# Pooling the first batch's keys with a 0/1 matrix of 32 columns in place of the identity

## The chip, the cores and the metric

The kernel runs on one core of a Trainium2 chip. A core has a matrix engine, TensorE (PE in the profile, with its loads of the stationary operand shown apart as PEld), three engines for elementwise work and reductions (VectorE or DVE, ScalarE or ACT, GpSimd or POOL) and sixteen DMA engines, whose transfers this kernel issues from SyncE's queue (SP). The engines run side by side, each in the order in which its instructions were written, and wait for each other through semaphores.

The metric is the device time of one execution. The kernel before takes 1979.55 us, the median of three runs from 1979.36 to 1980.42 us.

## The reference

```python
kv_pool = kv.reshape(B, H // r, r, W // r, r, C).mean(axis=(2, 4))     # r = 4
kv_flat = kv_pool.reshape(B, -1, C) @ w_sr
k = v = kv_flat
s = scale * (q @ k.transpose(0, 2, 1))
s = s - s.max(-1, keepdims=True)
a = np.exp(s); a /= a.sum(-1, keepdims=True) + 1e-09
x = (a @ v).reshape(B * S, D)
h = np.maximum(np.maximum(x @ w1, x @ w2), x @ w3)
out = h @ w_out
```

There are 4 batches. In each, kv is an image of 384 x 32 positions with 128 channels; every 4 x 4 block of positions is averaged, which leaves 96 x 8 = 768 pooled positions. They are projected by a 128 x 128 matrix and serve as keys and as values for 12288 queries. The attention's output (49152 rows of 128) goes through three 128 x 768 matrices, of which the largest value is taken, and through a 768 x 128 matrix. Softmax sums over all keys, so the order of the 768 pooled positions is free, as long as keys and values share it. The factor 1/16 of the mean is folded into scales.

## The kernel before, in words

The queries are worked in 96 groups of 512. For each group TensorE makes scores (`ps_s`), the weighted sum of the values (`ps_x`), six slices of hidden values (`ps_h`) and the output (`ps_o`), all as sums of float16 products; the other engines do softmax, maximum, splitting into float16 halves and scaling between them. Everything is issued by tables of tokens (`START`, `STEADY`, `END`), which are read from left to right; a token writes its instructions on whichever engines it needs. So each engine's order is the order of the tokens, and an instruction that waits holds back all that stands behind it on its engine. Line 105 is the helper through which every instruction is written, so the profile shows L105 for nearly all of them; tiles tell them apart.

The change concerns the keys of batch 0, which must be there before the first group can start. All of it stands in `START`:

- `kv.s.i` (`Keys.load`) brings a piece `kv_piece` of 512 KB. Three segments s of 32 pooled rows each are made from four pieces i. A piece holds, before, for 32 pooled rows h, the row number i of the four that are pooled together; a partition (h, w) has 8 neighbouring positions of that row, 4 KB, as two pooled columns u of four positions j with 128 channels each.
- `add.s.i.n` adds piece n to piece i on VectorE, in one instruction over 1024 elements a partition.
- `gat.s.i.4` and `end.s.i.4` (`Keys.gather`) take a piece into the accumulator of its segment in PSUM (segments 0 and 1 in a `ps_h` tile, segment 2 in a `ps_s` tile). For each u and j, eight in all, there is one float32 product with the 128 x 128 block of the piece as stationary operand and the identity `ident` as moving operand. That turns the block, channels to partitions, and the accumulation in PSUM adds up the positions j, the pieces i and both operands' halves. In the trace each of these products shows as two passes: two weight loads and two matmuls.
- `gathered_peak` takes the largest absolute value of a segment from PSUM on VectorE (`pool_max`), `gathered` copies the segment to `poolT` on ScalarE, `early_tops.1.2` combines the peaks of segments 1 and 2 and spreads them by a product with `ident` (`ps_h<-ident,pool_max`), `last_tops.0` does that for segment 0, and `gathered_project` multiplies by the projection (`ps_x<-poolT,wsr_sb`). Then follow the two float16 halves of the keys (`k_hi`, `k_lo`), and the first scores (`ps_s<-k_hi,qT`).

Segments 1 and 2 come first, segment 0 last. The keys of the other batches are pooled on VectorE in the shadow of other work (`keys_step`), and the change doesn't touch that. `kvp` has 13 buffers for pieces and raw weights, so the last loads wait until earlier ones are used up.

Of the kernel before, what the change touches and what calls it, by code (L numbers as in the profile page):

```python
# [9 lines left out]
F32 = mybir.dt.float32  # L10
# [6 lines left out]
ALU = mybir.AluOpType  # L17
AX = mybir.AxisListType
# [3 lines left out]
def kernel(  # L22
# [34 lines left out]
    R = 4  # L57
# [3 lines left out]
    P = 128  # L61
# [15 lines left out]
    KH, KW, KS, KU = 32, WB // 2, HB // 32, 2  # L77

    XB_ = 4
    const = ctx.enter_context(tc.tile_pool(name="const", bufs=1))  # L80
# [10 lines left out]
    op = ctx.enter_context(tc.tile_pool(name="op", bufs=2))  # L91
# [5 lines left out]
    class InOrder:  # L97
# [9 lines left out]
    pe, dve, act, pool, sp_dma = (  # L107
        InOrder(e) for e in (nc.tensor, nc.vector, nc.scalar, nc.gpsimd, nc.sync)
    )
# [5 lines left out]
    def spare(first):  # L115
        return ps_h.tile([P, G], F32, name="ps_h") if first else ps_x.tile([P, G], F32, name="ps_x")
# [8 lines left out]
    def times(t, src, by, by2=None):  # L125
# [4 lines left out]

    ident = const.tile([P, P], F32, name="ident")
    ones = const.tile([P, P], F32, name="ones")
    wsr_sb = const.tile([C, C], F32, name="wsr_sb")
    col_row = const.tile([P, C], F32, name="col_row")
    col = const.tile([C, 1], F32, name="col")
# [23 lines left out]
    SR_UP = 2.0 ** 10  # L159
    START = (  # L160
# [83 lines left out]
    class Weights64:  # L244
# [12 lines left out]
        def load(self):  # L257
            self.r1, self.r0 = load64(self.w, self.h, self.wide)
# [112 lines left out]
    class Keys:  # L371
# [17 lines left out]

        def load(self, s, i):  # L390
            piece = kvp.tile([P, PIECE], F32, name="kv_piece")
            src = kv[self.b].rearrange("(s h i) (w r) c -> s i h w (r c)", s=KS, i=R, w=KW)
            sp_dma.dma_start(out=piece, in_=src[s, i])
            self.pieces[s, i] = piece

# [15 lines left out]
        def gather(self, s, i, n, first, last, us=range(KU)):  # L411

            if first:
                self.acc[s] = spare(True) if s < 2 else two_banks()[:, 0]
            piece = self.pieces[s, i].rearrange("p (u j c) -> p u j c", u=KU, c=C)
            for u in us:
                for j in range(n):
                    mm(
                        out=self.acc[s][:, u * P:(u + 1) * P], lhsT=piece[:, u, j], rhs=ident,
                        start=first and u == 0 and j == 0, stop=last and u == KU - 1 and j == n - 1,  # L420
                    )

# [225 lines left out]
    def two_banks():  # L648
        return ps_s.tile([P, 2, G], F32, name="ps_s")
# [287 lines left out]
    sp_dma.dma_start(out=wsr_sb, in_=w_sr)  # L937
    make_identity(nc, ident)
    nc.vector.memset(ones, 1.0)
    warm = tiny.tile([P, 1], F32, name="warm", bufs=1)  # L940
    act.activation(out=warm, in_=ones[:, :1], func=AF.Exp)

# [205 lines left out]
```

## Time and profile before

| what | us |
|---|---|
| median of three runs | 1979.55 |
| span of the profiled execution, first to last instruction | 1977.9 |
| TensorE matmuls busy in the span | 1959.5 (99%) |
| VectorE, ScalarE, GpSimd busy | 1468.2, 1483.0, 1286.1 |

The profiled execution is one of its own, and its page gives its span, 1977.9 us, as its time; the 1.65 us between that and the median lie outside the first and the last instruction or between executions. TensorE is busy from 10 us to the end with almost no gap; its idle time, 18.4 us in all, lies in the first 70 us and at the very end. The granted-clock column of the page reads full speed in all slices, the first ones too.

How the times in the rows are read: a start is in us from the first instruction, followed by the time to the end of the last instruction of the merged row. Matmuls are pipelined, so the end of one lies some tenths of a us behind the start of the next; the pace of a series is the distance of starts.

### The profile page before, as it was taken

Reading aid. Unit: us, or ns where it says so; the run is one execution under the profiler, and the core shown is the slowest. Engines: PE = TensorE matmul, PEld = TensorE weight load, DVE = VectorE, ACT = ScalarE, POOL = GpSimd, SP = SyncE. Lnnn points to the kernel's source line nnn. Section 1 sums busy time; section 2 is a strip of 40 time slices with the busy share of each in tenths; the row PEclk is TensorE's granted clock in tenths of the full one; section 3 lists DMA queues with packets and bytes.
Section 4 is the critical chain, followed back from the end, with each engine's and each line's share of the span. In section 5 each row is a group of like instructions: output and inputs, shape, how many; then the busy total and the mean of one; then the engine's idle time right before and its main releaser. Section 6 shows DMA issues by size and latency. Waiting matters only on the chain.

```text
span 1977.9 us, 29533 instructions
## 1 busy us (share of the span) xinstructions
PE 1959.5 (99%) x9829; PEld 960.9 (49%) x9829; DVE 1468.2 (74%) x2554; ACT 1483.0 (75%) x2618; POOL 1286.1 (65%) x937
## 2 busy tenths in 40 slices
PE   7999999999999999999999999999999999999999
PEld 6444444444444444444444444444444444444444
DVE  6888987777667777777767777777767776766677
ACT  5876767777777777777777777777777777777775
POOL 3655456766666667766666666766676666666663
PEclk9999999999999999999999999999999999999999
DMA  9886677676678777767667778866677766766663
GB/s 282 164 167 134 129 163 136 135 142 138 125 148 169 155 149 163 135 135 142 132 127 167 154 147 161 165 126 132 137 139 141 126 127 127 147 121 126 133 128 81
DMA packets 845242, 284.60 MB, mean 144 GB/s; under 512 B 818721, under 2 KB 819873, under 8 KB 845089
## 3 DMA queue, kind: packets, MB, share of 16 engines
q1 hardware_dynamic: 845088, 282.71, 70.3%
q8 instruction: 77, 1.26, 0.3%
q14 instruction: 77, 0.62, 0.1%
HBM read 53.54 MB, written 25.17 MB: 40 GB/s over the span
## 4 chain that ended last, share of the span: by engine, by line
PE 96%; DMA 2%; POOL 1%; DVE 0%; issue 0%; ACT 0%; SPq 0%; DVEq 0%; POOLq 0%
PE ps_h L105 38%; PE ps_o L105 22%; PE ps_x L105 19%; PE ps_s L105 19%; DMA kv_piece<-in_kv_dram 1%; DMA aT<-ahl 0%; DMA qT<-q_hl 0%; POOL q_sb L105 0%; DMA o_turned<-o_planes 0%; POOL ahl L105 0%; POOL hl L105 0%; SPq L105 0%; ACT a L105 0%; ACT q_abs L105 0%; DVE ahl L105 0%
## 5 line engine op out<-in xcount | busy, mean ns | idle before, releaser
L105 POOL TENSOR_TENSOR hl<-h,hh 128x512 f16<-128x512 f32 x464 | 557.4, 1207 | 513.4 <-ACT hh L105 511.6
L105 POOL TENSOR_TENSOR ahl<-a,ahl 128x768 f16<-128x768 f32 x372 | 619.2, 1683 | 125.3 <-ACT ahl L105 76.5
L105 DVE SCALAR_TENSOR_TENSOR h<-ps_h,h 128x512 f32<-128x512 f32 x574 | 395.8, 690 | 346.8 <-PE ps_h L105 193.2
L105 ACT ACTIVATE h<-ps_h 128x512 f32<-128x512 f32 x574 | 342.2, 596 | 285.9 <-PE ps_h L105 276.3
L105 PE MATMUL ps_h<-xh,d_hi 128*128 128x512 f16 x1148 | 435.1, 379 | 0.2 <-DVE h L105 0.2
L105 PE MATMUL ps_h<-xl,d_hi 128*128 128x512 f16 x1148 | 435.1, 379 | 0.0
L105 PE MATMUL ps_h<-xh,d_lo 128*128 128x512 f16 x1148 | 435.1, 379 | 0.0
L105 DVE TENSOR_REDUCE mx<-ps_s 128x1 f32<-128x768 f32 x384 | 365.5, 952 | 52.1 <-PE ps_s L105 51.7
L105 ACT ACTIVATE a<-ps_s,nb,q_sc 128x768 f32<-128x768 f32 x384 | 379.2, 988 | 6.6 <-DVE nb L105 6.4
L105 PE MATMUL ps_s<-k_hi,qT 128*128 128x384 f16 x1536 | 374.8, 326 | 2.9 <-ACT a L105 2.6
L105 PE MATMUL ps_x<-aT,v_hi 128*128 128x512 f16 (+1 forms) x1188 | 367.2, 373 | 0.9 <-DMA aT<-ahl 0.9
L105 ACT CAST hh<-h 128x512 f16<-128x512 f32 x577 | 336.5, 614 | 40.4 <-DVE h L105 39.1
L105 PEld LDWEIGHTS <-d_hi 128*128 128x128 f16 x2308 | 225.8, 98 | 256.8 <-issue 0.3
L105 PE MATMUL ps_o<-hh,wo 128*128 128x512 f16 x1140 | 339.1, 379 | 0.0
L105 PEld LDWEIGHTS <-qT 128*128 128x128 f16 x2304 | 225.1, 98 | 192.0 <-issue 4.0
L105 ACT CAST ahl<-a 128x768 f16<-128x768 f32 x366 | 299.2, 829 | 8.5 <-DMA aT<-ahl 3.1
L105 PEld LDWEIGHTS <-wo 128*128 128x128 f16 x1710 | 167.3, 98 | 191.7
L105 PE MATMUL ps_s<-k_lo,qT 128*128 128x384 f16 x768 | 250.4, 326 | 0.0
L105 PE MATMUL ps_x<-aT,v_lo 128*128 128x512 f16 (+1 forms) x594 | 220.2, 373 | 0.0
L105 PE MATMUL ps_o<-hl,wo 128*128 128x512 f16 x570 | 216.0, 379 | 0.0
L105 PEld LDWEIGHTS <-v_hi 128*128 128x128 f16 x1188 | 115.5, 98 | 135.6 <-issue 1.5
L105 PEld LDWEIGHTS <-d_lo 128*128 128x128 f16 x1154 | 112.9, 98 | 121.8 <-issue 1.6
(149 smaller groups left out, 1450.5 us busy)
## 6 DMA issues: line engine op xcount, KB each, us to landing
q_sb<-in_q_dram SPq DMA_DIRECT2D x48, 512.0 KB, 4.3
kv_piece<-in_kv_dram SPq DMA_DIRECT2D x48, 512.0 KB, 4.4
out_dram<-o_sb SPq DMA_DIRECT2D x95, 256.0 KB, 2.0
aT<-ahl SPq DMA_TRANSPOSE x384, 4.0
kv_piece<-in_moe_w_dram SPq DMA_DIRECT2D x6, 384.0 KB, 7.7
qT<-q_hl SPq DMA_TRANSPOSE x96, 3.6
o_turned<-o_planes SPq DMA_TRANSPOSE x95, 3.4
kv_piece<-in_moe_w_out_dram SPq DMA_DIRECT2D x2, 384.0 KB, 9.7
```

Of the source, the lines that this page charges most:

```text
L105: return lambda **kw: tc.keep_in_program_order(op(**kw))
```

## The change

A table `fours` of 128 x 32 is made once: column (h, w) has a one in the four partitions (h, 0..3, w) and zeros elsewhere. It is a sum over groups of four of the identity's columns, on VectorE. A piece of batch 0 now is 32 whole rows of the image, 512 KB in one stretch, so that the four rows that are pooled together lie in four groups of partitions of the same piece. `gather` multiplies each of the eight blocks by `fours` in place of `ident`, which gives 32 columns instead of 128, and piece i with column u has a stretch of 32 of the accumulator's 256 columns to itself. The three `add` tokens go, and the three pieces that they swallowed get a `gat` of their own: nine gathered pieces become twelve. The order of the pooled positions changes, which softmax doesn't see.

```diff
+    fours = const.tile([P, P // R], F32, name="fours")
...
-        "wm.0.0 add.1.1.2 wd.1.0 qd qc kv.2.3 wm.1.0 qc gat.2.2.4 add.2.0.1 gat.1.1.4 gat.2.0.4 kv.1.3 wm.2.0",
+        "wm.0.0 wd.1.0 qd qc kv.2.3 wm.1.0 qc gat.2.2.4 gat.1.1.4 gat.1.2.4 gat.2.0.4 gat.2.1.4 kv.1.3 wm.2.0",
...
-        "wd.2.1 wt.0.0 wd.3.1 gat.0.1.4 wt.1.0& wm.2.1 wm.3.1 gat.0.0.4 wd.3.0 early qu ql wm.3.0 add.0.2.3 ql",
+        "wd.2.1 wt.0.0 wd.3.1 gat.0.3.4 gat.0.1.4 wt.1.0& wm.2.1 wm.3.1 gat.0.0.4 wd.3.0 early qu ql wm.3.0 ql",
...
-            src = kv[self.b].rearrange("(s h i) (w r) c -> s i h w (r c)", s=KS, i=R, w=KW)
+            if self.first:
+                src = kv[self.b].rearrange("(s i h) (w r) c -> s i h w (r c)", s=KS, i=R, w=KW)
+            else:
+                src = kv[self.b].rearrange("(s h i) (w r) c -> s i h w (r c)", s=KS, i=R, w=KW)
...
+                    at = (i * KU + u) * (P // R)
                     mm(
-                        out=self.acc[s][:, u * P:(u + 1) * P], lhsT=piece[:, u, j], rhs=ident,
+                        out=self.acc[s][:, at:at + P // R], lhsT=piece[:, u, j], rhs=fours,
                         start=first and u == 0 and j == 0, stop=last and u == KU - 1 and j == n - 1,
                     )
...
+    dve.tensor_reduce(
+        out=fours.rearrange("p (h w) -> p h w", w=KW), in_=ident.rearrange("p (h i w) -> p h w i", i=R, w=KW),
+        axis=AX.X, op=ALU.add,
+    )
```

TensorE's first instructions before, from the first piece to the last tops. A name stands as out<-moving,stationary; one row counts float32 products, each of which the trace shows as two passes.

```order
L105 MATMUL ps_h<-ident,kv_piece 128x128 x8
L105 MATMUL ps_s<-ident,kv_piece 128x128 x8
L105 MATMUL ps_h<-ident,kv_piece 128x128 x8
L105 MATMUL ps_s<-ident,kv_piece 128x128 x16
L105 MATMUL ps_h<-ident,kv_piece 128x128 x8
L105 MATMUL ps_h<-ident,pool_max 128x128
L105 MATMUL ps_h<-ident,kv_piece 128x128 x24
L105 MATMUL ps_h<-ident,pool_max 128x128
```

The same stretch of TensorE's order after the change:

```order
L105 MATMUL ps_h<-fours,kv_piece 128x32 x8
L105 MATMUL ps_s<-fours,kv_piece 128x32 x8
L105 MATMUL ps_h<-fours,kv_piece 128x32 x16
L105 MATMUL ps_s<-fours,kv_piece 128x32 x24
L105 MATMUL ps_h<-fours,kv_piece 128x32 x8
L105 MATMUL ps_h<-ident,pool_max 128x128
L105 MATMUL ps_h<-fours,kv_piece 128x32 x32
L105 MATMUL ps_h<-ident,pool_max 128x128
```

The 72 products of 128 columns become 96 of 32 columns: 64 instead of 48 ahead of the early tops, and 32 instead of 24 between the early and the last tops.

VectorE's order at the first two sums, with the row of difference:

```order
 L105 TENSOR_SCALAR q_up<-q_row 128x1
 L105 RECIPROCAL q_up<-q_up 128x1
-L105 TENSOR_TENSOR kv_piece<-kv_piece 128x1024 x2
 L105 TENSOR_SCALAR w_e<-w_e 128x384 x3
 L105 SCALAR_TENSOR_TENSOR w_e<-kv_piece,w_e 128x384 x3
```

The two sums are gone from between the scale of the first queries and the work on raw weights; the third is gone in the same way from between the two `q_hl` subtractions.

## Rows read from the trace of the kernel before

**Rows 1.** The profile's page: its head

```profile
span 1977.9 us, 29533 instructions
```

**Rows 2.** Stretches: us, busy us (x instructions) of PE, PEld, DVE, ACT, POOL; clock; DMA

```profile
10.00:20.00 10.00, 9.71 (x64) 9.55 (x64) 4.97 (x10) 1.02 (x2) 1.19 (x1) 1.00 1.03 412
...
100.00:1900.00 1800.00, 1799.79 (x8870) 867.56 (x8869) 1333.32 (x2294) 1370.32 (x2407) 1200.25 (x870) 1.00 0.70 141
```

**Rows 3.** The chain of waits, 10 to 72 us: start, us, what

```profile
10.11 9.92 DMA kv_piece<-in_kv_dram
...
20.07 2.05 PE ps_s L105 x16
...
24.96 5.86 PE ps_h L105 x50
30.84 0.44 DVE pool_max L105
...
70.58 0.97 PE ps_s L105 x6
```

**Rows 4.** TensorE's timeline, 10 to 33 us: start, us, shapes, xcount, [idle before <-releaser]

```profile
10.23 3.76 PE L105 MATMUL ps_h<-ident,kv_piece 128*128 128x128 f32 x16 [5.35 <-DMA kv_piece<-in_kv_dram]
13.78 2.59 PE L105 MATMUL ps_s<-ident,kv_piece 128*128 128x128 f32 x16
16.20 1.95 PE L105 MATMUL ps_h<-ident,kv_piece 128*128 128x128 f32 x16
17.98 4.14 PE L105 MATMUL ps_s<-ident,kv_piece 128*128 128x128 f32 x32
21.96 1.95 PE L105 MATMUL ps_h<-ident,kv_piece 128*128 128x128 f32 x16
24.96 0.49 PE L105 MATMUL ps_h<-ident,pool_max 128*128 128x128 f32 x2 [1.05 <-DVE pool_max L105]
25.28 5.52 PE L105 MATMUL ps_h<-ident,kv_piece 128*128 128x128 f32 x48
...
31.64 1.03 PE L105 MATMUL ps_x<-poolT,wsr_sb 128*128 128x256 f32 x4
```

**Rows 5.** TensorE's timeline of 11.3 to 13.3 us

```profile
11.00 2.55 PE L105 MATMUL ps_h<-ident,kv_piece 128*128 128x128 f32 x11
```

**Rows 6.** TensorE's groups of 11.3 to 13.3 us: xcount | busy us, mean ns | idle

```profile
L105 PE MATMUL ps_h<-ident,kv_piece 128*128 128x128 f32 x11 | 2.6, 421 | 0.0
```

**Rows 7.** Passes with one column: two at 4.3 us, two at 42.4 us

```profile
4.30 0.37 PE L105 MATMUL ps_h<-ones,col_row 1*128 1x1 f32 x1 [0.65 <-DVE col_row L105]
4.53 0.35 PE L105 MATMUL ps_h<-ones,col_row 1*128 1x1 f32 x1
...
42.38 0.27 PE L105 MATMUL ps_h<-d_top,col_ones 128*128 128x1 f32 x1
...
42.52 0.25 PE L105 MATMUL ps_h<-d_top,col_ones 128*128 128x1 f32 x1
```

**Rows 8.** VectorE's timeline: its first wait, a sum, a reduction, segment 0's peak

```profile
2.57 0.23 DVE L105 TENSOR_SCALAR sr_e<-wsr_sb 128x128 int32<-128x128 int32 x1 [1.57 <-DMA wsr_sb<-in_w_sr_dram]
...
13.95 1.22 DVE L105 TENSOR_TENSOR kv_piece<-kv_piece 128x1024 f32<-128x1024 f32 x1 [3.55 <-DMA kv_piece<-in_kv_dram]
...
25.48 0.29 DVE L105 TENSOR_REDUCE least<-ps_h 128x1 f32<-128x128 f32 x1
...
30.84 0.42 DVE L105 TENSOR_REDUCE pool_max<-ps_h 128x1 f32<-128x256 f32 x1 [1.27 <-PE ps_h L105]
```

**Rows 9.** SyncE's queue at 16.6 to 17.2 us: the issue of the last piece

```profile
16.55 0.54 SPq L105 DMA_DIRECT2D kv_piece<-in_kv_dram  x1
```

**Rows 10.** DMA issues of 16.5 to 17.2 us, the last piece: count, KB, us to landing

```profile
kv_piece<-in_kv_dram SPq DMA_DIRECT2D x1, 512.0 KB, 9.9
```

**Rows 11.** TensorE's waits from 31 to 100 us: total us, times, longest

```profile
PE ps_s L105 <- ACT a L105: 2.6, 3, 1.7
PE ps_x L105 <- DMA aT<-ahl: 0.9, 2, 0.5
```

## The prediction

> **What bounds the kernel now.** I read the page's head first: one execution, 1977.9 us from first to last instruction [rows 1]. The median of the runs shown is 1979.55 us, 1.65 us more; I make the sum on the profiled execution and add it to the median. Next the stretches: from 100 to 1900 us TensorE is busy for 1799.79 of 1800 us [rows 2]. From there on the kernel is TensorE's work without a gap, and the other engines run in its shadow. So a change in the start is worth what it does to the moment at which this stream of work can begin, plus what it adds to TensorE. That the moment isn't caught up later follows from the order: every engine works its table from left to right, and all that follows the pooling hangs on it.
>
> Then the chain of waits. Up to 20.0 us it is transfers of pieces; from 20.07 us it is TensorE's gathering, and the last part, 5.86 us for 50 passes, ends where VectorE takes the peak of segment 0 at 30.84 us [rows 3]. VectorE waited 1.27 us for it [rows 8]. So at the end the pooling is bound by TensorE, not by VectorE and not by the transfers: the last piece is issued at 16.55 us and takes 9.9 us [rows 9, 10], so it is there at 26.45 us.
>
> Last, TensorE's timeline in that stretch [rows 4], to be read by the distance of starts. A row of x16 is one piece, eight products of two passes. From 16.20 to 17.98 us a piece takes 1.78 us, 0.111 us a pass. The first piece takes 3.55 us (10.23 to 13.78). Inside it, eleven passes span 2.55 us [rows 5], the last of them 0.421 us long [rows 6], so the ten distances are 0.213 us each. The granted-clock column shows 1.00 here as everywhere [rows 2], but the same pass of the same shape takes 1.9 times as long: I take the passes up to about 15 us to have run at the lower of TensorE's two levels, 1.2 GHz, and the rest at 2.4 GHz. The pace doubles inside the second piece (16 passes in 2.42 us). By then TensorE had streamed 128-column passes without a gap since 10.23 us.
>
> **The change part by part.**
>
> *Three sums on VectorE go*: 3 x 1.22 us [rows 8]. None is in the chain of waits, and VectorE waits for TensorE at the end of the pooling anyway. Worth nothing.
>
> *`fours` is made once*: a reduction over 128 elements of a partition, 0.29 us [rows 8], in a stretch in which VectorE sat idle for 1.57 us. Without that cover it would cost 0.29 us ahead of a step that isn't in the chain either. Nothing.
>
> *The pieces are loaded as whole rows*: twelve transfers of 512 KB as before, 4 KB to a partition as before. If they came slower, the last piece would have to be later than its use to matter, and that use moves later by what follows, so some 7 us are free; if faster, only the first piece counts, for which TensorE waits. I take nothing, with 0.3 us to either side. In the queue two of the last loads now wait for other readers of their buffers; the same 7 us cover that.
>
> *144 passes become 192*: 12 pieces x 8 products x 2 passes instead of 9 x 16. What does a pass of 32 columns cost? The trace has none. Bounds: by columns alone, four passes of 256 columns give 0.217 us each at the fast pace (1.03 us less the 0.38 us of the last, over three distances) [rows 4], so 32 columns would take 0.027 us. From the other side, passes with a single column: two at 42.4 us end 0.12 us apart (42.38 + 0.27 and 42.52 + 0.25), two at 4.3 us end 0.21 us apart [rows 7]. That is the distance of passes with 128 columns, at either level. So a pass is as long as the load of its 128 x 128 float32 block, whatever streams through it, and that load is the same for `fours` as for the identity. I take 0.111 us fast and 0.213 us slow, the row with the narrower moving operand.
>
> The Trainium skill ("TensorE: Matmul & The Clock Gate", section "LDWEIGHTS (loading the stationary operand)") times a load by the columns of the stationary operand, 128 / 1.2 = 107 ns, an estimate from that page; the trace's 0.111 us agrees. The same page's table in "Back-to-back issue gap" gives matmuls of 1 to 64 columns about 25 ns; by that rule the gathering would be far cheaper (the third case below), and the single-column rows speak against it here.
>
> *The sum at an unchanged clock.* 48 more passes x 0.111 = 5.3 us. TensorE waited for a piece between 17.98 and 21.96 us: 3.98 us for 32 passes that need 3.55, so 0.4 us, which the longer queue swallows. The gap ahead of the early tops stays. Net +4.9 us: 1984.5 us.
>
> *The clock.* Before, the pace doubled after some 5 us of passes whose columns filled them. A pass of `fours` streams its columns in 0.027 of 0.111 us (0.05 of 0.21 us when slow) and is a load for the rest. No row shows the level rising under such passes. I hold it likelier that it does not, and stays at 1.2 GHz until the scores' float16 passes of 384 columns follow each other. Then: 192 x 0.213 = 40.9 us from 10.23 us, plus 0.14 us by which the first piece exceeds 16 distances, plus the gap and the early tops (the last pass of segment 1 should end its place at 21.96 + 1.78 = 23.74 us, the tops start at 24.96: 1.22 us; the two tops passes take 0.32 us fast, 0.5 us slow). The gathering's place ends at 10.23 + 40.9 + 0.14 + 1.22 + 0.5 = 53.0 us. Before it ended at 25.28 + 48 x 0.111 = 30.6 us. That is +22.4 us. Behind it, the passes up to the first scores run slow too: six of 256 columns and five of 128 cost 6 x 0.217 + 5 x 0.10 = 1.8 us more, and the six passes of the first tile, 0.97 us [rows 3], another 0.97 us. If the level takes two more tiles to rise, 2 us are added; against that, TensorE before waited 2.6 us there for the exponentials and 0.9 us for transposes [rows 11], which slower scores partly fill. I take +2.5 us, between 0 and +5. Sum 22.4 + 2.5 = +24.9 us, 2004.5 us, between 2002 and 2007.
>
> The Trainium skill (the same page, section "What's actually happening") says that the throttled level is TensorE's default and that activity releases it. The trace agrees as far as the slow pace stands at the start and the fast one ever after; no run here shows what narrow passes do.
>
> **The rivals.**
>
> First, the clock rises as before, because loads follow each other without a gap just as they did: 1984.5 us. For it: TensorE's queue has no more holes than before. If the rise comes some passes later, each slow pass adds 0.10 us, so 1985 to 1999 us lie between.
>
> Second, the forecast above: 2004.5 us.
>
> Third, on the other side: the load of the next block hides behind something that the single-column rows (pairs, not a long series) don't show, and a pass gets near its columns' 0.027 us. It decides below about 0.081 us a pass: from 16.20 us on 162 passes would have to fit into 30.6 - 16.20 - 1.22 = 13.2 us. The price is limited by the last piece at 26.45 us, and 16 x 0.027 = 0.4 us behind it: 26.9 in place of 30.6 us, -3.7 us, 1975.8 us. Against it stand four rows of one-column passes at two levels.
>
> Fourth, the transfers of whole rows come so much later that they bound the end. They would need 7 us; the pieces move the same bytes. I give it almost nothing.
>
> **How the numbers follow.** The clock stays low: 0.52. It rises as before: 0.34; somewhere between: 0.06. Cheap passes: 0.05. Anything else: 0.03. The predicted time is the likeliest case's, 2004.5 us. The range must reach to the first rival, since that case is too likely to leave out: 1983.9 to 2007.0 us. What a measurement can tell from no change is 0.2%, 1975.6 to 1983.5 us. The low clock, the first rival and what lies between are slower than that; the first rival by only 1 us, so some of it may fall inside. Cheap passes fall inside by little. Slower 0.90, same 0.07, faster 0.03.
>
> **What the profile of the changed kernel would show.** The passes on `fours` come in rows of x16 per piece, 192 in all. At an unchanged clock their distance drops from 0.213 to 0.111 us at some 15 us and the peak of segment 0 is taken near 35.8 us; in the forecast it stays at 0.213 us to the last piece, the peak is taken near 53 us and the first scores near 57 us, and the stretch from 100 us on is as full as before. VectorE waits for TensorE several us ahead of that peak. I am wrong if a pass takes far less than 0.11 us, if TensorE waits for pieces behind 21 us, or if the later stretches gain idle time or lose it.

## The result, and the profile after

The changed kernel takes 2003.66 us, the median of four runs (2003.42 to 2004.26), against 1979.47 us for the kernel before, timed beside it (1979.36 to 1980.42). The ratio is 1.0121, with a 95% interval from 1.0108 to 1.0133: 24.2 us slower. The forecast was 2004.5 us.

The head of the page of the kernel after; it answers to [rows 1]:

```profile
span 2001.6 us, 29624 instructions
```

The span has grown by 23.7 us. Next two stretches of the kernel after, with the columns of [rows 2]: us, busy us (x instructions) of PE, PEld, DVE, ACT and POOL, clock, DMA:

```profile
10.00:20.00 10.00, 10.00 (x48) 10.00 (x49) 2.87 (x7) 0.99 (x2) 1.54 (x2) 1.00 1.03 414
...
100.00:1900.00 1800.00, 1799.88 (x8874) 868.12 (x8872) 1340.86 (x2297) 1369.73 (x2407) 1202.14 (x869) 1.00 0.71 142
```

The long stretch is as full as before, 1799.88 against 1799.79 of 1800 us: nothing is lost or won there, so all of the difference must be made in the first 100 us. In the first stretch TensorE is busy without a gap, but it gets through 48 passes in 10 us, where before it got through 64.

The chain of waits of the kernel after (start, us, what), against [rows 3]:

```profile
3.08 6.64 DMA kv_piece<-in_kv_dram
...
9.76 3.62 PE ps_h L105 x16
13.38 3.41 PE ps_s L105 x16
...
23.62 10.24 PE ps_s L105 x48
...
38.41 14.27 PE ps_h L105 x66
...
52.71 0.44 DVE pool_max L105
```

Before, transfers led the chain up to 20.07 us. Now the first piece is the only transfer in it up to the peak of segment 0; from 9.76 us to that peak at 52.71 us it is TensorE's gathering with one short break. The gathering ends at 38.41 + 14.27 = 52.68 us, before at 24.96 + 5.86 = 30.82 us [rows 3]: 21.9 us later.

TensorE's timeline of the kernel after (start, us, shapes, xcount, [idle before <-releaser]), against [rows 4]:

```profile
9.76 3.62 PE L105 MATMUL ps_h<-fours,kv_piece 128*128 128x32 f32 x16 [4.89 <-DMA kv_piece<-in_kv_dram]
13.19 3.60 PE L105 MATMUL ps_s<-fours,kv_piece 128*128 128x32 f32 x16
16.60 7.01 PE L105 MATMUL ps_h<-fours,kv_piece 128*128 128x32 f32 x32
23.43 10.43 PE L105 MATMUL ps_s<-fours,kv_piece 128*128 128x32 f32 x48
33.67 3.60 PE L105 MATMUL ps_h<-fours,kv_piece 128*128 128x32 f32 x16
38.41 0.77 PE L105 MATMUL ps_h<-ident,pool_max 128*128 128x128 f32 x2 [1.14 <-DVE pool_max L105]
38.97 13.70 PE L105 MATMUL ps_h<-fours,kv_piece 128*128 128x32 f32 x64
53.19 0.80 PE L105 MATMUL ps_h<-ident,pool_max 128*128 128x128 f32 x2 [0.52 <-DVE pool_max L105]
53.78 1.91 PE L105 MATMUL ps_x<-poolT,wsr_sb 128*128 128x256 f32 x4
...
56.98 1.27 PE L105 MATMUL ps_s<-k_hi,qT 128*128 128x384 f16 x4
58.08 0.51 PE L105 MATMUL ps_s<-k_lo,qT 128*128 128x384 f16 x2
58.43 0.49 PE L105 MATMUL ps_s<-k_hi,qT 128*128 128x384 f16 x2
```

Count passes and distances: 16 + 16 + 32 + 48 + 16 + 64 = 192. From 16.60 to 23.43 us 32 passes take 6.83 us, 0.2134 us each; from 23.43 to 33.67 us 48 take 10.24 us, 0.2133 us each. The pace of the first piece before, 0.213 us [rows 5, 6], now holds to the last piece, and never doubles. One such pass lasts 401 ns, as the group of passes from 14 to 16 us says (xcount | busy us, mean ns | idle):

```profile
L105 PE MATMUL ps_s<-fours,kv_piece 128*128 128x32 f32 x12 | 2.7, 401 | 0.0
```

There is no wait for a piece behind the first one. The projection runs at the low pace too: four passes in 1.91 us, before in 1.03 us [rows 4]. The first four passes of scores take 1.10 us (56.98 to 58.08), but the two from 58.43 us end within 0.49 us: the fast pace is back inside the first tile of scores. The trace's own records of the granted clock agree: they begin at 57.8 us, with full speed, and in the kernel before at 15.1 us. Ahead of its first record the clock column reads 1.00 for want of one, so it can't show the low level there.

VectorE's peak of segment 0 in the kernel after, against [rows 8]:

```profile
52.71 0.42 DVE L105 TENSOR_REDUCE pool_max<-ps_h 128x1 f32<-128x256 f32 x1 [10.72 <-PE ps_h L105]
```

It waited 10.72 us for TensorE, before 1.27 us. The three sums that it no longer makes would have fallen into such idle time.

### The profile page after: what moved, and what is told of

Same layout as the page of the kernel before. It is cut to its first block, busy times and chain, and to the rows that moved or that the text cites. A ratio compares the mean times of both kernels' runs of the same rounds, so it can differ in the third digit from the quotient of the medians.

```text
span 2001.6 us, 29624 instructions
## 1 busy us (share of the span) xinstructions
PE 1983.7 (99%) x9877; PEld 985.2 (49%) x9877; DVE 1469.2 (73%) x2552; ACT 1482.7 (74%) x2618; POOL 1288.3 (64%) x937
## 4 chain that ended last, share of the span: by engine, by line
PE 97%; DMA 1%; DVE 1%; SPq 0%; ACT 0%; issue 0%; POOL 0%; ACTq 0%; DVEq 0%
PE ps_h L105 38%; PE ps_o L105 21%; PE ps_s L105 19%; PE ps_x L105 19%; DMA aT<-ahl 0%; SPq L105 0%; DMA kv_piece<-in_kv_dram 0%; DMA out_dram<-o_sb 0%; DVE mx L105 0%; ACT a L105 0%; DVE w_e L105 0%; DVE o_sb L105 0%; ACT ahl L105 0%; POOL ahl L105 0%; DVE nb L105 0%
```

## The experiments

All are timed against the kernel before, each with kernels of its group on the same chip; ratios carry their 95% intervals. My theory is the forecast's: 48 more passes cost some 5 us, each as long as its load, and the low level of the clock the rest. The rivals: something else in the changed kernel (the loads, the order of the pieces) makes the loss; narrow passes are cheap once the level is high; a high level stays high under them; a pass has a fixed length whatever it loads.

**More passes, nothing narrow.** The kernel before with its own pieces and the identity, but without the sums: twelve gathered pieces, 192 passes of 128 columns.

```diff
-        "wm.0.0 add.1.1.2 wd.1.0 qd qc ... gat.2.2.4 add.2.0.1 gat.1.1.4 gat.2.0.4 kv.1.3 wm.2.0",
+        "wm.0.0 wd.1.0 qd qc ... gat.2.2.4 gat.1.1.4 gat.1.2.4 gat.2.0.4 gat.2.1.4 kv.1.3 wm.2.0",
...
```

> The pieces and the identity of the kernel before, but without the three sums: twelve pieces are gathered in 192 passes of 128 columns, in the token order of the changed kernel. My theory (a pass is as long as its weight load, and the clock stays low because narrow passes hardly use the array): the pace doubles near 15 us as before, the gathering ends 4.9 us later than before, 1984.4 us. Rival 1 (the low clock has to do with the number of passes, the missing sums or the order of tokens, not with the columns): the pace stays at 0.213 us, about 2003.7 us. Rival 2 (the missing sums on VectorE matter by themselves): less than 1979.5 us.

Measured: 1984.49 us (1983.63 to 1985.79), ratio 1.0024 [1.0014, 1.0034]. The 48 extra passes cost some 5 us (2.8 to 6.7 us by the interval), and the three sums, which go with the same edit, were worth nothing that shows beside them.

**The changed kernel with a wide moving operand.** The 32 columns of `fours` stand in a table with zeros on either side, and each product streams 128 columns of it: 96 of zeros and 32 that count. Pieces, loads, order and number of passes are those of the changed kernel.

```diff
...
+                    if True:
+                        base = at // P * P
+                        out, rhs = self.acc[s][:, base:base + P], wide[:, P - P // R - at + base:2 * P - P // R - at + base]
                     mm(
-                        out=self.acc[s][:, at:at + P // R], lhsT=piece[:, u, j], rhs=fours,
+                        out=out, lhsT=piece[:, u, j], rhs=rhs,
...
```

> The changed kernel with one thing different: the moving operand of each pooling pass is 128 columns wide, the 32 columns of the 0/1 matrix among 96 columns of zeros, which add nothing to the sums. Same pieces, same 192 passes, same order. My theory: the pace doubles near 15 us, and the time falls by some 19 us to 1984.4 us, though each pass streams four times the columns. Rival 1 (columns don't matter for the clock): 2003.7 us. Rival 3 (only columns with other values than zero count for the clock): 2003.7 us too, but then the run without sums is at 1984.4 us.

Measured: 1984.26 us (1983.1 to 1986.06), ratio 1.0024 [1.0014, 1.0033]. TensorE's timeline of this run:

```profile
9.71 3.46 PE L105 MATMUL ps_h<-wide,kv_piece 128*128 128x128 f32 x16 [4.86 <-DMA kv_piece<-in_kv_dram]
13.01 1.95 PE L105 MATMUL ps_s<-wide,kv_piece 128*128 128x128 f32 x16
14.80 3.74 PE L105 MATMUL ps_h<-wide,kv_piece 128*128 128x128 f32 x32
...
27.12 7.31 PE L105 MATMUL ps_h<-wide,kv_piece 128*128 128x128 f32 x64
```

The same 192 loads, the same pieces: with four times the columns, three quarters of them zeros, the second piece already takes 1.79 us (13.01 to 14.80) instead of 3.41. A pass that streams four times as much is half as long. So the loss of the changed kernel falls into two parts: 1984.26 - 1979.64 = 4.6 us for the passes, against the kernel before of the same group, and the rest of the 24.2 us, 19.6 us, for the level at which they run. The whole-row pieces themselves cost nothing that shows: this run and the one before differ by 0.2 us.

**Wide first, narrow later.** Segments 1 and 2 with the wide operand, segment 0 with `fours`. The level is high when the narrow passes begin.

```diff
...
+                    if s > 0:
+                        base = at // P * P
+                        out, rhs = self.acc[s][:, base:base + P], wide[:, P - P // R - at + base:2 * P - P // R - at + base]
...
```

> The changed kernel with the 128-column operand for segments 1 and 2 and the 32-column one for segment 0 alone: 128 wide passes, then 64 narrow ones. It prices a narrow pass at the high level. My theory: 0.111 us a pass as long as the level holds, and 1984.4 us if it holds to the end of the 64 passes; each pass after a fall costs 0.10 us more, at most 6.5 us, 1991 us. Rival 4 (a narrow pass is cheap once the clock is high): 0.027 to 0.06 us a pass, so 3 to 5 us less, 1979 to 1981 us.

Measured: 1989.23 us (1988.93 to 1989.78), ratio 1.0047 [1.003, 1.0064]. Two groups of its passes on `fours`, from 28.2 to 30.8 us and from 32 to 38 us (xcount | busy us, mean ns | idle):

```profile
L105 PE MATMUL ps_h<-fours,kv_piece 128*128 128x32 f32 x25 | 3.0, 276 | 0.0
...
L105 PE MATMUL ps_h<-fours,kv_piece 128*128 128x32 f32 x30 | 6.6, 401 | 0.0
```

and the stretch from 31.2 to 38.5 us, columns as above:

```profile
31.20:38.50 7.30, 7.30 (x37) 7.30 (x36) 0.00 (x0) 0.00 (x0) 0.00 (x0) 0.50 0.62 142
```

This is the run that shows the level itself: the clock column reads 0.50, 1.2 GHz, in a stretch in which TensorE was busy all the time, with narrow passes and nothing else. The passes there last 401 ns, as those of the kernel after do, and come (6.6 - 0.4) / 29 = 0.21 us apart. So 401 ns and 0.213 us are the low level's, though the column stands at 1.00 in the start of the kernels before and after, ahead of its first record. Ahead of the fall the same passes last 276 ns and come (3.0 - 0.28) / 24 = 0.11 us apart, as wide ones do. A narrow pass is no cheaper than a wide one at either level, and under narrow passes the level fell. The gap of 1.14 us ahead of the early tops does not explain the fall: the run with wide passes alone has the same gap, and its level stayed high. Segment 0 alone so costs 1989.23 - 1984.26 = 5.0 us.

**Fillers ahead of the changed kernel.** 24 products of 256 float16 columns before the first piece, into a tile that nobody reads.

```diff
-        "wd.0.0 qd sr wd.0.1 wd.2.0 qc qc kv.1.0 gat.1.0.4 wm.0.1 ...
+        "wd.0.0 qd sr wd.0.1 wd.2.0 warm.24 qc qc kv.1.0 gat.1.0.4 wm.0.1 ...
```

> The changed kernel with 40 or fewer idle products in front, 24 of 256 float16 columns on the identity, from some 4.9 us to the first piece, so that TensorE streams full passes before the narrow ones. My theory: the level may rise, but narrow passes don't keep it for long; then the time lies near 2003.7 us, less 0.10 us for each pass run at the high level. Rival 5 (narrow passes can't raise the level but hold it once it is up): all 192 run at 0.111 us, the gathering ends near 33 us, 1982 us. If the fillers end before the level rises, the run says nothing on this, and the time is as without them.

Measured: 2003.5 us (2003.03 to 2005.24), ratio 1.0121 [1.0106, 1.0136]: no gain that shows. TensorE's timeline and two stretches of this run:

```profile
9.84 1.87 PE L105 MATMUL ps_h<-fours,kv_piece 128*128 128x32 f32 x16
12.30 2.91 PE L105 MATMUL ps_s<-fours,kv_piece 128*128 128x32 f32 x16 [0.59 <-DMA kv_piece<-in_kv_dram]
15.03 7.01 PE L105 MATMUL ps_h<-fours,kv_piece 128*128 128x32 f32 x32
...
51.55 0.80 PE L105 MATMUL ps_h<-ident,pool_max 128*128 128x128 f32 x2 [0.52 <-DVE pool_max L105]
...
74.53 0.27 PE L105 MATMUL ps_x<-aT,v_hi 128*128 128x128 f16 x1 [1.58 <-DMA aT<-ahl]
```

```profile
13.00:20.00 7.00, 7.00 (x36) 7.00 (x35) 2.32 (x4) 0.99 (x2) 1.57 (x2) 0.51 1.03 410
20.00:50.00 30.00, 28.95 (x137) 28.82 (x136) 6.65 (x17) 4.95 (x11) 3.49 (x3) 0.50 0.48 156
```

The first piece is gathered fast, in 1.87 us, but then TensorE waits for the second, and inside it the level falls and stays at 0.50 until the scores. In the kernel after the level did not rise under the narrow passes; here, raised ahead of them, it didn't last. What the fillers won on the first piece was not lost in the gathering: the last tops start at 51.55 us, 1.64 us earlier than in the kernel after. It was lost later. In this execution TensorE waits 1.58 us ahead of 74.53 us for transposed softmax weights (`aT`), the clock column reads 0.50 again from 74.6 to 77.9 us, and the span is 2003.5 us, 1.9 us longer than that of the kernel after. In the medians a gain of 1.6 us would be too small to be told.

**Half blocks.** Each product of the changed kernel is cut into two, one for each half of 64 channels, still on the 32 columns of `fours`: 384 passes, each with half the load.

```diff
-                    mm(
-                        out=self.acc[s][:, at:at + P // R], lhsT=piece[:, u, j], rhs=fours,
...
+                    for c in (slice(0, 64), slice(64, 128)):
+                        mm(
+                            out=self.acc[s][c, at:at + P // R], lhsT=piece[:, u, j, c], rhs=fours,
...
```

> The changed kernel with each pooling product cut in two along the channels: twice as many passes, each with a stationary block of 64 columns instead of 128 and the same 32 moving columns. My theory (the weight load sets the length of a pass): a half block loads in half the time, 0.107 us at the low level, the 384 passes take what the 192 took, and the time stays at 2003.7 us if the level stays low. If twice the moving columns in the same time are enough to raise the level, it falls towards 1984.4 us. Rival 6 (a float32 pass has a fixed length, whatever is loaded): 192 more passes x 0.213 = 41 us, 2044.6 us.

Measured: 1985.99 us (1984.7 to 1986.42), ratio 1.0031 [1.0019, 1.0043]. The forecast was missed by 18 us; that the time lies near 1984.4 us, the price of a level that rises, is chance, as the rows show. TensorE's timeline:

```profile
9.25 1.92 PE L105 MATMUL ps_h<-fours,kv_piece 128*64 128x32 f32 x32 [4.29 <-DMA kv_piece<-in_kv_dram]
...
26.02 7.04 PE L105 MATMUL ps_h<-fours,kv_piece 128*64 128x32 f32 x128
33.59 0.79 PE L105 MATMUL ps_h<-ident,pool_max 128*128 128x128 f32 x2 [0.53 <-DVE pool_max L105]
34.18 1.91 PE L105 MATMUL ps_x<-poolT,wsr_sb 128*128 128x256 f32 x4
```

Four pieces stand in the row at 26.02 us: 128 passes in 7.04 us, less the 0.3 us of the last, give 0.053 us a pass, 0.106 us a pair. I had expected a half load to take half as long, and a pair as long as a whole block: 0.213 us at the low level. A pair takes half of that. The level is not what changed: the last tops (0.79 us) and the projection (1.91 us) right behind have the lengths that they have in the kernel after. The starts in the trace come in pairs: two passes start 0.007 us apart, and the next two 0.107 us behind them. So the two halves go side by side, and the time of one pair is that of one half. A fixed length per pass is ruled out too, since 384 passes took less time than 192.

**Early tops behind a piece.** In the kernel before, TensorE waits 1.05 us ahead of the early tops [rows 4]. Here one more piece is gathered in that place, and the third sum comes earlier.

```diff
-        "wr.1.0 ... wl.2.0 wr.2.0 qh early_tops.1.2",
-        "wd.2.1 wt.0.0 wd.3.1 gat.0.1.4 wt.1.0& ... early qu ql wm.3.0 add.0.2.3 ql",
+        "wr.1.0 ... wl.2.0 wr.2.0 qh",
+        "wd.2.1 wt.0.0 wd.3.1 gat.0.1.4 early_tops.1.2 wt.1.0& ... early qu add.0.2.3 ql wm.3.0 ql",
```

> The kernel before (identity, three sums) in another order: the product of the early tops stands behind the first gathered piece of segment 0 instead of ahead of it, and the third sum ahead of the two subtractions of the queries' halves. TensorE's idle stretch before the early tops (1.05 us) is then filled by that piece. My theory: the gathering, which bounds the start, ends about 1 us earlier and the whole kernel with it, 1978.5 us. Rival 7 (the start isn't bound there): 1979.5 us, no change.

Measured: 1979.12 us (1978.41 to 1982.32) against 1979.06, ratio 1.0000 [0.9992, 1.0009]. No gain shows, though one of 1 us would lie inside the interval. TensorE's timeline says where it went:

```profile
13.76 3.11 PE L105 MATMUL ps_s<-ident,kv_piece 128*128 128x128 f32 x16
16.70 1.95 PE L105 MATMUL ps_h<-ident,kv_piece 128*128 128x128 f32 x16
...
28.50 2.05 PE L105 MATMUL ps_h<-ident,kv_piece 128*128 128x128 f32 x16 [0.53 <-DVE kv_piece L105]
31.06 0.49 PE L105 MATMUL ps_h<-ident,pool_max 128*128 128x128 f32 x2 [0.52 <-DVE pool_max L105]
```

The gap moved: TensorE now waits 0.53 us for the last sum on VectorE. And in this execution the fast pace came later: the second piece takes 2.94 us (13.76 to 16.70), before 2.42 us [rows 4]. The projection behind the last tops starts at 31.39 us, 0.25 us earlier than before [rows 4], too little to be told in the time. So this run doesn't decide between the theory and the rival.

**Half blocks with 64 columns.** The half blocks again, with 64 moving columns (32 of them zeros) so that more is streamed in a pass, and the early tops behind two pieces. A second kernel has the 24 fillers besides.

```diff
...
+                    base = at // WIDE * WIDE
+                    shift = WIDE - P // R - at + base
+                    for c in (slice(0, 64), slice(64, 128)):
+                        mm(
+                            out=self.acc[s][c, base:base + WIDE], lhsT=piece[:, u, j, c], rhs=wide[:, shift:shift + WIDE],
...
```

> The half blocks of 64 stationary columns, whose passes ran in pairs at 0.107 us a pair at the low level, with moving operands of 64 columns (the 0/1 matrix and 32 columns of zeros), and the product of the early tops behind two gathered pieces of segment 0. My theory (the two halves load and stream side by side, and a pass is as long as the longer of load and stream; more columns in the same time may raise the clock): if the level rises near 15 us, 0.053 us a pair, a piece takes 0.85 us, the gathering is bound by the last piece's landing at 26.45 us and ends near 27.4 us instead of 30.6: 1976.3 us. If the level stays low, a piece takes 1.7 us, TensorE ends near 31.6 us and the passes behind it are slow too: 1984.8 us. Rival 8 (the two halves only load side by side and stream one after the other): twice as long, 1.7 us a piece at the high level: 1980 us.

> The same with 24 filler products of 256 float16 columns ahead of the first piece, which raised the level at 9.7 us when they stood in front of the narrow passes. My theory: the level is high from the first piece on; if the 64-column halves hold it, the gathering ends near 27.4 us, 1976.3 us, and no sooner than without fillers, since the pieces' landing bounds it; if they don't hold it, as without fillers.

Measured: 1981.47 us (1980.29 to 1982.97), ratio 1.0006 [0.9997, 1.0015], and with fillers 1980.92 us (1980.33 to 1984.09), ratio 1.0006 [0.9996, 1.0015], both against 1979.97 us. Neither beats the kernel before, and the 1976.3 us of the expectations were missed by some 5 us. TensorE's timeline of the run with fillers, and two stretches of it:

```profile
10.08 1.15 PE L105 MATMUL ps_h<-wide,kv_piece 128*64 128x64 f32 x32
...
20.40 1.98 PE L105 MATMUL ps_s<-wide,kv_piece 128*64 128x64 f32 x32 [2.76 <-DMA kv_piece<-in_kv_dram]
...
26.03 2.09 PE L105 MATMUL ps_h<-wide,kv_piece 128*64 128x64 f32 x64
30.35 0.80 PE L105 MATMUL ps_h<-ident,pool_max 128*128 128x128 f32 x2 [2.23 <-DVE pool_max L105]
```

```profile
20.20:23.20 3.00, 2.80 (x52) 2.80 (x54) 2.65 (x3) 0.93 (x1) 3.00 (x3) 0.50 1.04 410
23.50:30.00 6.50, 4.62 (x142) 4.29 (x137) 4.31 (x14) 3.40 (x8) 1.00 (x1) 1.00 1.14 366
```

Here both levels of the half blocks are on record. The row at 20.40 us lies in the stretch with the clock at 0.50: 32 passes in 1.98 us, some 0.11 us a pair, as I had read from the run before. At 1.00 a piece takes 1.15 us, some 0.06 us a pair, so the halves stream side by side as well; rival 8 had 1.7 us a piece at this level. TensorE is now so quick that it waits for pieces again, 2.76 us ahead of 20.40 us, and right behind that wait the level is low.

The gathering ends near 28.1 us (26.03 + 2.09), 2.7 us earlier than before. Yet the last tops start at 30.35 us, because TensorE waits 2.23 us for the peak. VectorE's timeline of this run shows why:

```profile
29.60 0.36 DVE L105 TENSOR_SCALAR w_e<-w_e 128x384 int32<-128x384 int32 x1 [0.76 <-ACT w_e L105]
29.88 0.42 DVE L105 TENSOR_REDUCE pool_max<-ps_h 128x1 f32<-128x256 f32 x1
```

The peak could start at 28.1 us but stands behind two shifts of raw weights, and the second of them waits 0.76 us for ScalarE. The bound of the start has moved from TensorE's gathering to VectorE's queue, and behind the 2 us of idle TensorE the level is low once more (the last tops take 0.80 us, as at the low level).

That is not the whole loss. The first scores, and the stretch from 60 to 100 us, each in the kernel before and then in the run with fillers:

```profile
33.47 1.01 PE L105 MATMUL ps_s<-k_hi,qT 128*128 128x384 f16 x4
33.88 0.49 PE L105 MATMUL ps_s<-k_hi,qT 128*128 128x384 f16 x2
...
60.00:100.00 40.00, 39.25 (x194) 18.66 (x193) 33.57 (x57) 31.18 (x57) 25.95 (x18) 1.00 0.77 150
60.00:100.00 40.00, 37.39 (x178) 17.48 (x176) 31.90 (x52) 29.04 (x54) 24.56 (x18) 0.96 0.71 138
```

The first scores start only 0.41 us later than before, but the span of this execution, the slowest of the eleven, is 4.4 us longer. From 60 to 100 us TensorE gets through 178 passes in place of 194: it waits 2.6 us for transposed softmax weights (`aT`), and behind that the level is low for a while. What brings this wait is not shown.

**The peak ahead of the weights.** The work on the last raw weights moves behind the peak and the copy of segment 0, on VectorE and ScalarE. The queries' work moves too: the two subtractions of their halves (`ql`) come earlier, a scale of theirs (`qu`) later. Again without and with fillers; the diff is against the runs before.

```diff
-        "wr.1.0 ... gathered.1 wl.2.0 wr.2.0 qh",
-        "wd.2.1 ... early_tops.1.2 wt.1.0& wm.2.1 wm.3.1 gat.0.0.4 wd.3.0 early qu ql wm.3.0 ql",
-        "ws.2.1 wd.1.1 end.0.2.4 ws.3.1 qt gathered_peak.0 last_tops.0 wl.2.1 ws.3.0 tops gathered_project.1",
-        "first_sized gathered.0 qt ...
+        "wr.1.0 ... gathered.1 ql wl.2.0 wr.2.0 qh",
+        "wd.2.1 ... early_tops.1.2 ql wt.1.0& gat.0.0.4 wd.3.0 early",
+        "wd.1.1 end.0.2.4 qt gathered_peak.0 last_tops.0 tops gathered_project.1",
+        "first_sized gathered.0 wm.2.1 wm.3.1 wm.3.0 ws.2.1 ws.3.1 qu wl.2.1 ws.3.0 qt ...
```

> The half blocks with 64 columns (as in the run before it), and besides on VectorE and ScalarE the work on raw weights of the second half (the sums and shifts that wait for the last raw weights) moved behind the peak and the copy of segment 0. My theory: with half blocks the end of the pooling is no longer TensorE's gathering but VectorE's queue: the last pass was at 28.76 us and the last tops only at 30.99 us, since the peak stood behind shifts that wait for ScalarE and the raw weights. With these moved the peak follows the last pass by 0.2 us and the tops come near 29.4 us, 1.6 us earlier than in the half-block run; the level of the clock may then not fall in the gap, another 0.9 us. So 0.8 to 2.5 us under the half-block run: 1979 to 1980.5 us beside a kernel before of 1979.5 us, a ratio of 0.9995 to 1.0005. Rival: the moved work on weights is needed soon after (the first group's hidden products), the hole only moves there, and the time stays at the half-block run's 1.0006 or goes above it.

> The same with the 24 filler products of 256 float16 columns ahead of the first piece, so that the level is high when the first pieces come. Theory: last pass near 27.9 us, tops near 28.6 us, 2 us earlier than before's 30.6: a ratio of 0.9988 to 0.9998. Rival: the raw weights are late, the hole moves behind the first scores, and the ratio is 1.0000 to 1.0010.

Measured: 1982.79 us (1981.74 to 1983.56) and 1982.25 us (1981.54 to 1985.67) against 1980.01, ratios 1.0012 [1.0003, 1.0021] and 1.0014 [1.0005, 1.0023]. TensorE's timeline and one link of the chain of waits of the first:

```profile
29.86 0.49 PE L105 MATMUL ps_h<-ident,pool_max 128*128 128x128 f32 x2 [0.53 <-DVE pool_max L105]
...
34.29 1.46 PE L105 MATMUL ps_s<-k_hi,qT 128*128 128x384 f16 x4 [2.32 <-DMA qT<-q_hl]
```

```profile
25.74 8.50 DMA qT<-q_hl
```

The peak comes right behind the last pass, as expected, and the last tops start at 29.86 us, 1.5 us earlier than before. But now the first scores wait 2.32 us for the transposed queries. One of their two transfers took 8.50 us, where before the two took 4.5 and 5.4 us; it was issued at 25.74 us, before at 27.1 us, and why it took longer is not shown. Behind the wait the level is low again: the clock column reads 0.50 from 34.3 to 37.6 us. In this run the rival was right that the gap only moves, though not to where it said: it was the queries, not the weights' products. With fillers the first scores start at 33.43 us, as early as before, and the loss is made behind them: from 60 to 100 us TensorE again gets through 178 passes and waits 2.2 us for `aT`. Whether late raw weights, which the second rival named, stand behind that is not shown. No version that I ran beats the kernel before.

## Why the prediction was right

**The pooling was bound by TensorE, and what comes later shifts with it.** This held: the gathering ends 21.9 us later, the span grows by 23.7 us, and the stretch from 100 to 1900 us is as full as before. The experiments add a limit that the prediction did not name: the shift is rigid for delays only. When TensorE's gathering ends 2.7 us early, other chains, VectorE's queue and the transposed queries, take its place, later waits come on top (for `aT` with fillers; without them 1.4 and 1.5 us for the hidden values `h` between 100 and 200 us, before 0.2 us), and nothing is won.

**The sums, `fours` and the whole-row loads cost and bring nothing.** Held, as far as it can be told. The first product waits for its piece and not for `fours`; no product waits for a later piece. The first pass started at 9.76 us, 0.47 us earlier than before. I don't put that down to the whole rows: the first pass starts between 9.25 and 10.39 us in the executions with whole rows, between 9.98 and 10.23 us in those without, and the one spread covers the other.

**A pass costs its load, not its columns.** Held for whole blocks at both levels: 0.2134 us a pass at the low level, 0.111 us at the high one, with 32 columns as with 128. The table of the Trainium skill ("TensorE: Matmul & The Clock Gate", section "Back-to-back issue gap") with about 25 ns for narrow matmuls leaves out the load of the stationary operand, as the section says of its formula. So it was no price for these passes, which each bring a load and took 0.111 us. The term was +4.9 us; the two runs in which the level rose as before gave 4.9 and 4.6 us, with 2 us to either side, so the agreement to a tenth is luck. In their profiled executions the last tops start 4.0 and 3.6 us later than before, since there the first piece came earlier and the second already ran at the fast pace.

**The clock stays low.** Held, and it is the larger part: 19.6 of 24.2 us. The rows of before did not decide it, and the prediction gave it 0.52, so that the choice fell right was in part luck; the experiments decide it. In the two runs in which the level was high when the narrow passes began, it fell under them; in the run with the wide operand it rose under the same loads. The first rival was thus right in its price (1984.5 us, measured 1984.49) and wrong in its condition, that loads without a gap would do.

**The sizes.** For the gathering the sum said +22.4 us, and 21.9 us were measured; the difference is the earlier first piece. For the passes behind it the sum said +2.5 us, and 23.7 - 21.9 = 1.8 us were measured: the projections and tops cost what they were taken for, but the level rose inside the first tile of scores, so the 0.97 us for that tile were mostly not paid. On the profiled execution the sum, 24.9 us, was 1.2 us too high.

**What was wrong** lies outside the prediction. The expectation for the half blocks carried its step, that a pass is as long as its load, over to blocks of 64 columns, one load behind the other. The step holds for whole blocks; two halves overlap, and that expectation missed by 18 us.

## What to carry to other kernels

A matrix product that does less arithmetic can be slower for it: when each pass loads its own stationary block, narrowing the moving operand saves nothing, and a stretch of such passes may run at half the clock from end to end. Read the level from the distance of equal passes, not only from the clock column, and price the change at both levels before choosing. And when the bound of a start is relieved, look at once for the two or three chains that end within a microsecond or two of it: here a gain of 2.7 us in the gathering was eaten by VectorE's order first, by the transposed queries next, and by waits some 30 us and more behind the start.

## What the runs showed of the hardware that I had not expected

- Columns of zeros did as well as any: with 96 of 128 moving columns zero, the second piece was gathered at the high pace (1.79 us), and the level stayed high.
- Two products on the two halves of a stationary block, 64 columns each, run side by side: 0.106 us a pair at 1.2 GHz and some 0.06 us at 2.4 GHz, where one whole block takes 0.213 and 0.111 us. The Trainium skill ("TensorE: Matmul & The Clock Gate", section "The mechanism") describes concurrent tiles of the array and says that a load overlaps matmuls in flight only where the row groups differ. Here the rows are the same and only the columns differ, and the halves ran side by side all the same.
- The level fell more than once in the same start: in the run with half blocks and fillers it was high at 10 us, 0.50 from 20.2 to 23.2 us behind a wait of 2.76 us, and back at 1.00 from 23.5 us.
